# Moving an output layer's first sums and an x^T load to earlier places in a fused attention and squared-ReLU kernel

## The chip, the cores and the metric

The kernel runs on one core of a Trainium2 chip. The core has five engines with a queue each: TensorE (PE, matrix products), VectorE (DVE), ScalarE (ACT), GpSimd (POOL) and SyncE (SP, which here issues nearly all DMAs). Each engine takes its instructions strictly in the order in which the program gives them, and waits on semaphores for the others. The metric is device time in microseconds (us); lower is better.

## The reference

Two blocks one after the other, all in float32:

```python
scores = q @ k.T / 8                      # 8 x 8 heads, 576 positions, head size 64
scores = where(scores >= max(scores) - tau, scores, -1e9)
attn   = exp(scores - max) / (sum + 1e-9)
x      = (attn @ v), heads side by side   # 4608 x 512
h      = maximum(x @ w_in, 0)             # w_in 512 x 2048
out    = (h * h) @ w_out                  # w_out 2048 x 512, out 4608 x 512
```

## The kernel before

**Attention.** 32 pairs of heads, each cut into five blocks of queries, give 160 *slots*. `slot(n)` is a pipeline written out by hand: it mixes stages of several neighbouring blocks (scores of block n + 3, softmax of n + 1 and n + 2, transposes of n - 1, products with the values of n - 2). The result of a block is copied from PSUM by ACT (L418, L421) into one of three buffers `xr` and stored as x^T to DRAM by SP (queued in `later`, issued by `ask()`, L547). Between the slots of attention lie side jobs: from slot 0 the output weights are fetched and converted, from slot 35 POOL makes sums of them (`sums`, L130), which SP stores in groups of seven tiles (`keep`, also L547); from slot `IN_FIRST` = 76 the input weights follow (fetch at L181, conversion at L201 to L239). At slot 76 SP is also asked for x^T of the first token step, `load_x(0)` (L641, four DMAs of 256 KB), and from slot 78 on POOL makes one sum of it in every third slot (`prepare_x`, L130). That x^T lies in a region of its own.

**Both layers of the feed-forward part** use a Winograd form of Strassen's scheme two levels deep: 7 outer times 7 inner products for each step of 512 tokens (9 steps), 49 *products* of four matmuls. The price are sums and differences of blocks, before the products (of the operands) and after them (of the results). The outer loop runs over `OUTER` = (1, 2, 6, 7, 4, 5, 3); I call the place in that loop *index* 0 to 6. Within an index, `inner` makes seven products (1, 6, 7, 5, 2, 4, 3) into four PSUM banks out of a ring of six, with a *tick* after each (0 to 6):

```python
        product(X, 1, False); copy(p1, X);          tick(0)
        product(Y, 6, False); u2 = Y + p1;          tick(1)
        product(Z, 7, False); u3 = Z + u2;          tick(2)
        product(W, 5, False); final((1,1), W, u3);  tick(3)
        product(X, 2, True);  final((0,0), X, None); tick(4)
        product(Z, 4, True);  final((1,0), Z, u2);  tick(5)
        product(W, 3, True);  final((0,1), W, u2);  tick(6)
```

(shortened). The last three products add into banks that `p1`, `u3` and the first `final` must have read before.

*Hidden layer* (`hidden_layer`, products at L708): DVE makes the sums that read PSUM (L133); POOL makes a second addition for most results (L133, one for each of three results in an index, two in index 5). A finished block goes to ACT four ticks later: ReLU (L687), square (L688), and SP stores it to DRAM as `g` (L689).

*Output layer* (`output_layer`, products at L843): its operands are `g` blocks, loaded back by `load_g` (L786). Sums of them come in two kinds. `outer_sums(n, o, ks)` give the blocks (o, k) for outer products o = 5, 6, 3, 7; each is made by `sum_v`: ACT copies one operand to a PSUM bank `c` (L654), and DVE adds or subtracts (L133, L130). `inner_sums(n, m)` give (m, 5), (m, 6), (m, 3) on POOL and (m, 7) by `sum_v`. I write (5,7) for the outer sum with o = 5 and k = 7.

**The last step of the hidden layer** (n = 8) has no next x^T to prepare. It is used for step 0 of the output layer: `load_g(0, ...)` asks for the 16 blocks of m = 7, 4, 1, 2 at its start; a table `work` gives sums by index, and `spread(work, at)` spreads the list of an index over its seven ticks; in the same ticks `reload` (L940) brings the output weights back into the tiles of the input weights. In the output layer, `work_of(i)` gives the sums to be made during index i. The first copy of that layer, `p1` of index 0 (L622), goes into a buffer that was a hidden-layer `U2` block until POOL's last addition has read it.

Of the kernel before, what the change touches and what calls it, by code (L numbers as in the profile page):

```python
# [48 lines left out]
def kernel(  # L49
# [218 lines left out]
    def load(i):  # L268
        b, hp = pairs[i]
        h = 2 * hp  # L270
        qn = sb.tile([P, FULL, P], FP32, tag="qn", name="qn")
        kn = sb.tile([P, FULL, P], FP32, tag="kn", name="kn")

        rn = sb.tile([P, P], FP32, tag="rn", name="rn")

        for src, dst, order, rows in ((q, qn, "(t p) d -> p t d", 0), (k, kn, "(p t) d -> p t d", REST)):

            queue = nc.scalar if i == 0 and src is k else nc.sync
            for j in range(2):
                queue.dma_start(out=dst[:, :, ds(j * D, D)], in_=src[b, h + j, 0:MAIN, :].rearrange(order, p=P))  # L280
            queue.dma_start(
                out=rn[ds(rows, REST), :].rearrange("p (j d) -> p j d", j=2),
                in_=src[b, h : h + 2, MAIN:S, :].rearrange("j p d -> p j d"),
            )
        loaded[i] = (qn, kn, rn)
# [164 lines left out]
    def turn_part(n, part):  # L450

        if n < 0:
            return
        if n not in rows_of:
            transposes(n)
        rows_of[n][part]()
# [22 lines left out]
    def give_x(n, xr):  # L479
        i, t = slots[n]  # L480
        b, hp = pairs[i]
        later.append((xT[b][ts(hp, P), ds(t * P, BLK[t])], xr[:, 0, 0 : BLK[t]]))
# [51 lines left out]
    IN_FIRST = OUT_SUMS + 41  # L534
# [240 lines left out]
    def operand(n, m, k):  # L775
        at = PLACE[(28 * n + 4 * KINDS.index(m) + K_ORDER.index(k)) % 36]
        operands[n, m, k] = arena[:, ds(at, BANK)].rearrange("p (k t) -> p k t", k=4)
        return operands[n, m, k]

    def load_g(n, kinds):  # L780

        for m, k in kinds:
            row, col = next((a, b) for a in range(2) for b in range(2) if AT_A[a][b] == m)
            a, b = next((a, b) for a in range(2) for b in range(2) if AT_A[a][b] == k)
            j = 4 * (2 * col + b) + 2 * row + a
            nc.sync.dma_start(out=operand(n, m, k), in_=gT[n][j][:, :].rearrange("p (k t) -> p k t", k=4))  # L786
# [9 lines left out]
    def outer_g(n, o, k):  # L796
        op, x, y = SUM_OF[o]
        x, y = operands[n, x, k], operands[n, y, k]
        sum_g(nc.vector, op, operands[n, o, k] if o == 7 else operand(n, o, k), x, y)

    def inner_g(n, m, o):
        op, x, y = SUM_OF[o]
        x, y = operands[n, m, x], operands[n, m, y]
        if o != 7:
            operands[n, m, o] = fin.tile([P, 4, NQ], FP32, tag="gi")
        sum_g(nc.vector if o == 7 else nc.gpsimd, op, operands[n, m, o], x, y)

    def inner_sums(n, m):
        return [lambda o=o: inner_g(n, m, o) for o in (5, 6, 3, 7)]

    def outer_sums(n, o, ks=K_ORDER):
        return [lambda k=k: outer_g(n, o, k) for k in ks]
# [72 lines left out]
    with tc.manual_schedule():  # L885
        with ExitStack() as stack:
            sc_pool = stack.enter_context(tc.tile_pool(name="sc", bufs=2, space=PSUM))
            b_pool = stack.enter_context(tc.tile_pool(name="b", bufs=2, space=PSUM))

            def bank(shape, name):  # L890
                return b_pool.tile(shape, FP32, tag="b", name=name)

            def keep_busy(times):

                pt = bank([P, P], "idle")
                for _ in range(times):
                    nc.tensor.transpose(pt[:, :], ident[:, :], ident[:, :])

            load(0)
            load_v(0)  # L900
            keep_busy(10)
            for _ in turn(0):
                pass
            turn_last(0, bank([P, P], "pqkr")[:, :])()
            load_v(1)
            for n in range(-3, len(slots)):
                slot(n)
                if -3 < n < 0:
                    keep_busy(12)
                if n == IN_FIRST:  # L910
                    load_x(0)
                    xsums = prepare_x(0, lambda op, out, x, y: op(nc.gpsimd, out, x, y))
                if n > IN_FIRST + 1 and n % 3 == 0:
                    next(xsums, None)
            n = len(slots)

            def drain():

                while pending:
                    pt, m, of = pending.popleft()  # L920
                    xr = sb.tile([P, 2, P], FP32, tag="xr", bufs=3)
                    nc.scalar.copy(xr[:, 0, 0:m], pt[:, 0, 0:m])
                    give_x(of, xr)

            drain()
            values_and_load(n - 2)
            for part in "RWw":
                turn_part(n - 1, part)
            values_and_load(n - 1)
            drain()  # L930
            for _ in range(60):
                sums_step()
            ask()
        banks = ctx.enter_context(tc.tile_pool(name="banks", bufs=1, space=PSUM))

        def reload(at):

            m, k = OUTER[at // 7], INNER[at % 7]
            t = weight_tile(W_OUT, m, k)
            nc.sync.dma_start(out=t[:, :], in_=w_dram[m, k][:, :])  # L940

        for n in range(NSTEP):
            last = n == NSTEP - 1
            if not last:
                load_x(n + 1)
                xsums = prepare_x(n + 1, sum_v)
            else:
                load_g(0, [(m, k) for m in (7, 4, 1, 2) for k in K_ORDER])
                work = {
                    3: [*outer_sums(0, 5, (7,)), *outer_sums(0, 6, (7,))],  # L950
                    4: [*outer_sums(0, 3, (7,)), *outer_sums(0, 7, (7,))],
                    5: inner_sums(0, 1),
                    6: outer_sums(0, 5, (1, 2)) + outer_sums(0, 7, (1,)),
                }

            def also(m, at):
                i = OUTER.index(m)
                if not last:
                    if 2 <= i <= 5 and at < 6:
                        next(xsums)  # L960
                    return
                spread(work.get(i, []), at)
                if 7 * i + at > 9:
                    reload(7 * i + at - 10)

            hidden_layer(n, also)
            if not last:
                next(xsums, None)
        for n in range(NSTEP):
            more = n + 1 < NSTEP  # L970

            def work_of(i):

                work = [] if i == 6 else inner_sums(n, OUTER[i + 1])
                if (n, i) == (0, 0):
                    work += outer_sums(0, 6, (1, 2)) + outer_sums(0, 5, (4,)) + outer_sums(0, 6, (4,))
                if (n, i) == (0, 1):
                    work += outer_sums(0, 7, (2, 4)) + outer_sums(0, 3, (1, 2, 4))
                if more and i == 4:
                    work += outer_sums(n + 1, 5)  # L980
                if more and i == 5:
                    work += outer_sums(n + 1, 6) + outer_sums(n + 1, 7, (7, 1))
                if more and i == 6:
                    work += outer_sums(n + 1, 3) + outer_sums(n + 1, 7, (2, 4)) + inner_sums(n + 1, 1)
                return work

            def also(m, at):
                i = OUTER.index(m)
                if n == 0 and 7 * i + at < 10:
                    reload(39 + 7 * i + at)  # L990
                if more and (i, at) == (2 if n == 0 else 0, 0):
                    load_g(n + 1, [(m_, k) for m_ in KINDS[0:2] for k in K_ORDER])
                if at == 0:
                    work[0] = work_of(i)
                spread(work[0], at)
                if at > 4:
                    squares_due(0)
                if at == 2:
                    ask()
                if at == 6:  # L1000
                    if more and i == (2 if n == 0 else 0):
                        load_g(n + 1, [(7, k) for k in K_ORDER])
                    if more and i == (2 if n == 0 else 1):
                        load_g(n + 1, [(4, k) for k in K_ORDER])

            work = [None]
            output_layer(n, also)
        ask()
# [36 lines left out]
```

## Time and profile before

| | |
|---|---|
| median of 7 runs | 1465.62 us (1465.27 to 1467.18) |
| profiled execution | 1465.27 us, of it span 1463.5 us |
| PE busy | 1435.8 us, 98% of the span |
| POOL, DVE, ACT busy | 1053.2, 1007.1, 889.8 us |
| DMA | 176.90 MB, mean 121 GB/s |
| attention | 0 to 662.9 us |
| hidden layer | 662.9 to 1061.1 us, nine steps of 44 us |
| output layer | 1061.1 to 1460 us, nine steps of 44 us |

A busy time is the time in which the engine had an instruction under way. The stages follow one another on PE, and each has another set of helpers, so a wait has to be read in its own stage. "A <- B" in the profile means that A was released by B. In the tables of groups and waits, a line such as L133 is a helper's line (`plus`; `minus` is L130), so the tile names tell the uses apart: `ph` is a hidden-layer product, `po` one of the output layer, `arena` the big SBUF region, `c` the bank of `sum_v`.

### The profile page before, as it was taken

How to read it: one execution, taken by the hardware profiler on the slowest of the kernel's cores; microseconds unless marked ns; L12 is line 12 of the kernel's file. 1: busy time of each engine (PE TensorE's matmuls, PEld its weight loads, DVE VectorE, ACT ScalarE, POOL GpSimd, SP SyncE). 2: the span in 40 equal slices, each digit the busy share in tenths (PEclk: the TensorE clock that was granted, in tenths of full speed). 3: DMA queues.
4: the chain of work that ended last, by engine and by line, in shares of the span. 5: the costliest groups of instructions: out<-in, count | busy, mean ns of one | idle time of the engine just before them, and what ended most of it. 6: DMA issues, size and time to landing. Idle time of an engine off the chain costs nothing. (4 is left out here: it accounts for less than half of the span.)

```text
span 1463.5 us, 35324 instructions
## 1 busy us (share of the span) xinstructions
PE 1435.8 (98%) x12914; PEld 1216.1 (83%) x12914; DVE 1007.1 (69%) x2152; ACT 889.8 (61%) x1792; POOL 1053.2 (72%) x1318
## 2 busy tenths in 40 slices
PE   8999999999999999999999999999999999999998
PEld 5666666666666666669999999999999999999998
DVE  4888766777887667666777877777765666545663
ACT  5888777777887777774766665766553333322330
POOL 3777788878888888773556655566677777777775
PEclk9999999999999999999999999999999999999999
DMA  4343223566442222202433233433984432244411
GB/s 126 106 128 112 62 65 114 163 231 205 123 122 75 54 55 65 64 26 63 144 127 128 93 112 120 145 123 127 386 294 145 144 130 78 88 140 144 145 30 30
DMA packets 212957, 176.90 MB, mean 121 GB/s; under 512 B 99888, under 2 KB 161328, under 8 KB 212784
## 3 DMA queue, kind: packets, MB, share of 16 engines
q1 hardware_dynamic: 210896, 174.09, 37.6%
q8 instruction: 102, 1.67, 0.5%
q10 hardware_dynamic: 1888, 0.56, 0.2%
q14 instruction: 71, 0.58, 0.1%
HBM read 105.12 MB, written 69.47 MB: 119 GB/s over the span
## 5 line engine op out<-in xcount | busy, mean ns | idle before, releaser
L133 POOL TENSOR_TENSOR arena<-arena 128x512 f32<-128x512 f32 (+1 forms) x314 | 376.9, 1223 | 252.4 <-DVE arena L133 208.4
L708 PE MATMUL ph<-arena,w 128*128 128x128 f32 x3528 | 396.6, 275 | 2.1 <-DVE arena L133 1.1
L843 PE MATMUL po<-w,arena 128*128 128x128 f32 x3528 | 396.3, 275 | 2.1 <-ACT arena L622 1.8
L708 PEld LDWEIGHTS ph<-arena,w 128*128 128x128 f32 x3528 | 394.7, 192 | 4.0 <-DVE arena L133 3.5
L843 PEld LDWEIGHTS po<-w,arena 128*128 128x128 f32 x3528 | 394.7, 192 | 3.6 <-ACT arena L622 2.0
L133 DVE TENSOR_TENSOR arena<-ph,arena 128x512 f32<-128x512 f32 x378 | 255.7, 688 | 94.0 <-PE ph L708 53.4
L366 DVE TENSOR_REDUCE arena<-sc 128x1 f32<-128x576 f32 x288 | 217.5, 755 | 127.5 <-PE sc L355 127.3
L383 DVE SCALAR_TENSOR_TENSOR arena<-sc,arena 128x576 f32<-128x576 f32 x288 | 224.6, 814 | 7.2 <-ACT arena L378 7.0
L398 POOL TENSOR_SCALAR arena<-arena 128x576 f32<-128x576 f32 (+1 forms) x320 | 223.5, 708 | 7.4 <-DVE arena L389 2.6
L133 DVE TENSOR_TENSOR arena<-po,arena 128x128 f32<-128x128 f32 x378 | 108.2, 290 | 169.7 <-PE po L843 166.5
L654 ACT COPY c<-arena 128x512 f32<-128x512 f32 (+1 forms) x303 | 172.7, 579 | 61.5 <-DVE arena L130 56.4
L378 ACT ACTIVATE arena<-sc,arena 128x576 f32<-128x576 f32 x288 | 200.7, 747 | 10.6 <-DVE arena L366 6.4
L439 PEld LDWEIGHTS pwT<-ident,arena 128*128 128x128 f32 x1152 | 128.5, 141 | 77.0 <-issue 29.9
L355 PE MATMUL sc<-arena 64*128 64x512 f32 (+2 forms) x768 | 184.5, 571 | 1.1 <-DVE arena L383 0.7
L130 POOL TENSOR_TENSOR arena<-arena 128x512 f32<-128x512 f32 (+1 forms) x138 | 175.0, 1268 | 11.8 <-DMA arena<-xT 2.1
L439 PE MATMUL pwT<-ident,arena 128*128 128x128 f32 x1152 | 181.0, 280 | 1.2 <-ACT arena L311 0.7
L130 DVE TENSOR_TENSOR arena<-arena,c 128x512 f32<-128x512 f32 (+1 forms) x267 | 174.8, 663 | 6.9 <-ACT c L654 6.3
L441 ACT COPY arena<-pwT 128x512 f32<-128x512 f32 x256 | 151.4, 592 | 41.8 <-PE pwT L439 31.6
L469 PE MATMUL pvR<-arena 128*64 128x128 f32 (+1 forms) x2560 | 163.3, 268 | 5.1 <-ACT arena L441 0.7
L469 PEld LDWEIGHTS pvR<-arena 128*64 128x64 f32 x2560 | 127.8, 136 | 34.9 <-issue 20.6
L687 ACT ACTIVATE arena<-arena 128x512 f32<-128x512 f32 x144 | 89.9, 624 | 77.6 <-POOL arena L133 77.6
L622 ACT COPY arena<-po 128x128 f32<-128x128 f32 x63 | 16.7, 265 | 180.1 <-PE po L843 178.1
(56 smaller groups left out, 1157.0 us busy)
## 6 DMA issues: line engine op xcount, KB each, us to landing
g<-arena SPq DMA_DIRECT2D x144, 256.0 KB, 2.0
arena<-g SPq DMA_DIRECT2D x144, 256.0 KB, 4.3
w<-w SPq DMA_DIRECT2D x98, 256.0 KB, 4.8
out_dram<-arena SPq DMA_DIRECT2D x70, 128.0 KB, 2.3
arena<-in_q_dram SPq DMA_DIRECT2D x64, 128.0 KB, 2.6
arena<-in_v_dram SPq DMA_DIRECT2D x32, 256.0 KB, 2.8
arena<-in_moe_w_out_dram SPq DMA_DIRECT2D x16, 512.0 KB, 4.1
xT<-arena SPq DMA_DIRECT2D x128, 64.0 KB, 1.5
```

The lines of the kernel that those rows point to most:

```text
L130: e.tensor_tensor(out=out, in0=x, in1=y, op=ALU.subtract)
L133: e.tensor_tensor(out=out, in0=x, in1=y, op=ALU.add)
L355: nc.tensor.matmul(to, qT[rows, ds(t * P, m)], kT[rows, ds(k0, n)], start=True, stop=True)
L366: nc.vector.tensor_reduce(out=nmx[:, j : j + 1], in_=sc[:, ds(at[j], S)], axis=AXIS.X, op=ALU.max, negate=True)
L378: nc.scalar.activation(out=w[:, ts(j, S)], in_=sc[:, ds(at[j], S)], func=AF.Exp, bias=nmx[:, j : j + 1], scale=1.0)
L383: nc.vector.scalar_tensor_tensor(out=w[:, ts(j, S)], in0=sc[:, ds(at[j], S)], scalar=thr[:, j : j + 1], in1=w[:, ts(j, S)], op0=ALU.is_ge, ...
L398: nc.gpsimd.tensor_scalar(out=out, in0=w, scalar1=r, scalar2=1.0, op0=ALU.mult, op1=ALU.mult)
L439: nc.tensor.transpose(pt[:, c, :], w[:, ds(j * (S + REST) + c * P, P)], ident[:, :])
L469: nc.tensor.matmul(pv[rows, :], va[:, j, c, :], wT[:, j, c, 0:n], start=(c == 0), stop=False, skip_group_check=True)
L654: nc.scalar.copy(c, y)
L708: nc.tensor.matmul(to[:, j, :], W_IN[m, k][:, ts(j, P)], of[k][:, m - 1, :], start=(not more and j == 0), stop=True, skip_group_check=True,)
L843: nc.tensor.matmul(to, g[:, j, :], w[:, j, :], start=(not more and j == 0), stop=(j == 3), skip_group_check=True)
```

## The change

It has two parts. The load of the first step's x^T is asked for after slot 64 instead of after slot 76; the sums of it stay in their slots. And in the last hidden step the sums for output step 0 are placed anew: the four outer sums with k = 7 go from indices 3 and 4 to 2 and 3; the inner sums of m = 1 go from index 5 to 4; index 5 has none; in index 6, (5,1) and (5,2) stay at ticks 2 and 4, the entries `rest` being empty; (7,1) leaves index 6 for index 1 of the output layer, ahead of (7,2) and (7,4).

```diff
-                if n == IN_FIRST:
+                if n == IN_FIRST - 12:
                     load_x(0)
                     xsums = prepare_x(0, lambda op, out, x, y: op(nc.gpsimd, out, x, y))
...
                 load_g(0, [(m, k) for m in (7, 4, 1, 2) for k in K_ORDER])
+                rest = lambda: None
+                first, second_one = outer_sums(0, 5, (1, 2))
                 work = {
-                    3: [*outer_sums(0, 5, (7,)), *outer_sums(0, 6, (7,))],
-                    4: [*outer_sums(0, 3, (7,)), *outer_sums(0, 7, (7,))],
-                    5: inner_sums(0, 1),
-                    6: outer_sums(0, 5, (1, 2)) + outer_sums(0, 7, (1,)),
+                    2: outer_sums(0, 5, (7,)) + outer_sums(0, 6, (7,)),
+                    3: outer_sums(0, 3, (7,)) + outer_sums(0, 7, (7,)),
+                    4: inner_sums(0, 1),
+                    6: [rest, rest, first, rest, second_one, rest, rest],
                 }
...
                 if (n, i) == (0, 1):
-                    work += outer_sums(0, 7, (2, 4)) + outer_sums(0, 3, (1, 2, 4))
+                    work += outer_sums(0, 7, (1, 2, 4)) + outer_sums(0, 3, (1, 2, 4))
```

## The prediction

> **What bounds the kernel now.** I read the page first. TensorE (PE) is busy 1435.8 of 1463.5 us, at a granted clock of 0.9 or more in every slice, so no other engine's busy time buys anything; what can be won is PE's idle time, 27.7 us in all, and only where the changed lines cause it. Second, the waits of PE, whose columns are the total in us, the number of waits and the longest. I keep those that fall next to the edits.
>
> ```profile
> PE po L843 <- ACT arena L622: 1.8, 1, 1.8
> PE ph L708 <- DVE arena L133: 1.1, 1, 1.1
> PE pqk L306 <- ACT arena L418: 1.1, 1, 1.1
> PE pwT L439 <- ACT arena L311: 0.7, 1, 0.7
> PE pvR L469 <- ACT arena L309: 0.3, 1, 0.3
> ```
>
> Each occurs once. The first two lie at the seam of hidden and output layer (1059 to 1067 us), where the sums are moved; the other three follow each other within 7 us of attention (339 to 346 us), just after the load that is moved. Third, the timeline of both places (start, duration; in brackets the idle time before and its releaser). Around the load:
>
> ```profile
> 331.95 2.13 SPq L641 DMA_DIRECT2D arena<-xT  x4
> 334.49 0.33 SPq L547 DMA_DIRECT2D xT<-arena  x1
> 339.31 0.37 ACT L418 COPY arena<-pvR 128x256 f32<-128x256 f32 x1 [2.73 <-DMA xT<-arena]
> 339.74 0.66 PE L306 MATMUL pqk<-ident,arena 128*128 128x128 f32 x4 [1.09 <-ACT arena L418]
> 342.64 0.66 PE L439 MATMUL pwT<-ident,arena 128*128 128x128 f32 x4 [0.74 <-ACT arena L311]
> 346.06 0.69 PE L469 MATMUL pvR<-arena 128*64 128x64 f32 x16 [0.32 <-ACT arena L309]
> ```
>
> SP issues in order. The four loads of x^T (1 MB) stand ahead of an x^T store whose data ScalarE (ACT) had ready at 325.3. The store goes out at 334.49 and lands 4.7 us later, at 339.2; the `xr` ring has three buffers, so the copy that reuses that buffer (due at 339.31 - 2.73 = 336.58) stands still for 2.73 us, and PE loses 1.09 + 0.74 + 0.32 = 2.15 us while ACT catches up. Around the seam:
>
> ```profile
> 1056.92 0.63 ACT L687 ACTIVATE arena<-arena 128x512 f32<-128x512 f32 x1 [0.56 <-POOL arena L133]
> 1058.12 0.58 ACT L654 COPY c<-arena 128x512 f32<-128x512 f32 x1
> 1058.81 0.69 DVE L133 TENSOR_TENSOR arena<-arena,c 128x512 f32<-128x512 f32 x1 [1.74 <-ACT c L654]
> 1060.15 1.16 PE L708 MATMUL ph<-arena,w 128*128 128x128 f32 x8 [1.13 <-DVE arena L133]
> 1060.60 0.63 ACT L687 ACTIVATE arena<-arena 128x512 f32<-128x512 f32 x1 [1.90 <-POOL arena L133]
> 1066.37 0.27 ACT L622 COPY arena<-po 128x128 f32<-128x128 f32 x1 [2.00 <-POOL arena L133]
> 1066.68 3.50 PE L843 MATMUL po<-w,arena 128*128 128x128 f32 x29 [1.80 <-ACT arena L622]
> ```
>
> This is one chain, read from the top: a late GpSimd (POOL) add holds a ReLU on ACT; the copy to `c` for an output-layer sum queues behind it; VectorE (DVE) waits for `c` with the hidden layer's own sum behind it; PE waits 1.13. The same again, then POOL's last add frees the buffer of the first `p1` copy of the output layer, and PE waits 1.80. POOL is late because in index 5 (m=5) it has six adds of its own and three inner sums: 9 x 1.25 = 11.2 us in an index of seven products of 44.01 / 49 = 0.898, 6.3 us.
>
> **The change part by part.** No instruction is added or taken away; the eleven sums of the work table keep their operations, nine of them move. Each DVE sum is an ACT copy (0.55 to 0.59) and a DVE operation (0.62 to 0.69), each POOL sum 1.25.
>
> *The load.* Four DMAs leave SP at slot 76 and enter at slot 64, with a slot of 4.0 us. On the changed SP queue they stand behind a group of seven weight stores (273.81 to 277.67) and before two x^T stores. Removed at 332: the store goes out at 331.95 instead of 334.49, with 1 MB less in front of it. This case's ordinary x^T stores land in 1.5 to 2.7 us, so at 333.5 to 334.7, and even the 4.1 us of a crowded store gives 336.1, before 336.58. The stall goes: -2.15. POOL's first x^T sum, which waited 2.1 us for this load, no longer waits; PE did not wait for that. Added at 277.8: SP is blocked for 2.1 to 2.5 us; the store now issued at 277.77 goes out at about 280.2, behind the rest of the weight stores (the DMA engines are busy until 279.5) and 1 MB more at some 380 GB/s, 2.8 us, so it lands near 282.3 + 2 = 284.3. Its buffer is wanted three copies later, at 288.81: 4.5 us to spare. The next store (issued about 281) needs to land by 293.0. SP then waited until 284.58 for the v load, 3.2 us after it was through, so the q, k and v loads are not moved. Cost 0.
>
> Here two rules speak, one against the edit. The Trainium skill, "DMA: Bandwidth & Descriptors", section "Anatomy of one DMA — SWDGE (gpsimd) path", gives a DMA about 2.0 us of constant fixed cost plus its bytes over 436 GB/s. The page fits it for GpSimd's path, but taken as the law for a 32 KB store, it would land at 334.49 + 2.1 = 336.6, ACT would not have waited, and moving the load would be worth 0. The row says 4.7 us, because the store's data wait behind the loads; the row decides, and the sum has 2.15. In the same page, section "Queues, rings and completion order", descriptors are consumed in ring order: that is the reason why the stores behind the load at slot 64 must pay too, 2.8 us each as used above. By that rule the stall could simply move; by the rows of that place it has 4.5 us of room.
>
> *The sums.* In index 2 now come (5,7) and (6,7), in index 3 (3,7) and (7,7), in index 4 the inner sums, in index 5 none, in index 6 as before (5,1), (5,2) at ticks 2 and 4, while (7,1) goes to index 1 of the output layer.
> - Index 5: POOL has 6 x 1.25 = 7.5 us instead of 11.2. Index 4 takes 6 x 1.25 = 7.5 as well, on a POOL that idled 2.00 us there. It starts index 5 on time (1052) and has the (1,0) output ready at about 1055.9 instead of 1056.9, the (0,1) output at 1058.4 instead of 1060.58.
> - First wait: ACT has the ReLU at 1056.36, the moment it is free, instead of 1056.92. Copy, sum and PE follow 0.56 sooner: 1.13 becomes 0.57. It does not go, since (5,1) and (5,2) stay where they are.
> - Second wait: ReLU and square of (0,1) run from 1058.7 to 1059.9; `c` for (5,2) is there at 1060.4 (before: 1062.4), the DVE sum at 1061.0, the product sums at 1061.7 and 1062.3, POOL's two adds until about 1064.4, the `p1` copy until 1064.7. PE, started 0.56 sooner, ends its four products at 1064.3 and goes on at about 1064.6 instead of 1066.68. So the second wait becomes 0.3, and PE is 2.1 us earlier in all.
> - Cover of the sums moved up: at tick 3 of index 2 ACT is still in squares until 1033.72, so `c` is ready at 1034.2 and the sum at 1034.9; five DVE operations behind it run until 1038.6, and PE's product that needs the last of them starts at 1039.3. 0.7 us remain; if that cover is gone, PE pays the excess. The operands are there: the 16 g loads go out from 1018.7 to 1028.1 and land in 2.9 to 6.0 us; the latest one needed in index 2 is the ninth.
> - Index 1 of the output layer gets a seventh copy and sum, 0.55 on ACT and 0.62 on DVE. In the trace of before the next `p1` copy ends at 1078.15 and is needed at 1079.25; DVE is level again at 1079.8, and PE needs it at 1081.0. Both hold 0.6 more. Cost 0, up to 0.5 if I misread an order.
> - SP's queue keeps its order in the last step; the reload of weights (DMA busy share 1.05 until 1073) runs some 30 us ahead of its use.
>
> Bounds, per edit: the load between +1 (a new stall of half the size) and -3.0 (the three waits and a wait of 0.91 at 356.5 on DVE, which I count as staying: there POOL has an x^T sum, a conversion and two small copies in a row). The sums between +0.5 and -2.93 (both waits gone). Sum taken: -2.15 - 2.1 = -4.25. Profiled execution: 1465.27 (span 1463.5 and 1.8 around it), so 1461.0; the median of the runs is 0.35 above the profiled one, so 1461.4.
>
> **The rivals.**
> 1. Only one edit pays. Either the store stall comes from the crowd of weight stores and q, k, v loads on SP and not from x^T (for: those alone held SP from 321.45 to 331.9; against: 331.95 plus 4.1 is in time), or the seam's waits only change their releaser. Then 1463.2 to 1463.5.
> 2. Both pay fully, the 0.91 with them, and the first seam wait vanishes: -2.15 - 0.9 - 2.9 gives 1459.7.
> 3. Slower: the new place of the load makes a store stall of its own. Place: the ACT copy at 288.8. Price: PE paid 2.15 for an ACT wait of 2.73, so 0.8 per us. It decides once the store lands after 288.8, and outweighs the gains (4.25 / 0.8 = 5.3 us) only if it lands after 294.1, nearly 14 us after its issue, or if the old stall stays too (2.1 / 0.8 = 2.6 us, landing after 291.4). The longest landing seen near is 5.6 us. Then about 1466.
> 4. The edit does nothing in effect, because PE gives the time back at the next tight place: no later PE wait in the output layer is listed, so PE has nothing to give it back to.
>
> **How the numbers follow.** A difference under 0.2% (2.9 us) is about what a measurement of this kernel can't tell from no change. Forecast (gain 3 to 5.2): 0.62. Rival 2: 0.10. Rival 1: 0.18, within 0.2%. Rival 3: 0.06; rival 4: 0.04. Faster by over 0.2%: 0.62 + 0.10 = 0.72; the same: 0.18 + 0.04 = 0.22; slower: 0.06. The range from 1459.8 to 1463.6 takes in the forecast, most of rival 2 and rival 1.
>
> **What would show it.** Right: no ACT wait on an x^T store near 336, four L641 issues near 278, hidden layer beginning 2.1 us sooner (662.9 to 660.8); in the seam, index 5 on POOL without a subtraction, PE's wait on L708 at 0.6 and on L843 at 0.3. Wrong: an ACT wait on xT near 289, a PE wait on L708 in indices 2 to 4, a PE wait on L843 in index 2 of the output layer, or the 339 us waits still there.

## The result, and the profile after

The changed kernel takes 1461.58 us (median of 15 runs, 1461.13 to 1462.13) against 1465.59 us of the kernel before, measured with it (35 runs). The ratio is 0.9972, 95% interval 0.9965 to 0.9978: 4 us less. The profiled execution has a span of 1460.0 us, 3.5 less than before: the hidden layer begins 1.35 sooner (at 661.55 instead of 662.90), and from there to the end it takes 798.46 us instead of 800.58, 2.12 less. That execution was late from its first slots on: just ahead of the old stall the same product starts at 329.91 in it and at 329.37 before. The stretch from there to the hidden layer is 1.9 shorter.

First the waits of PE in the changed kernel, those next to the edits (total in us, number, longest; the view lists waits of 0.15 us and more):

```profile
PE ph L708 <- DVE arena L133: 0.5, 1, 0.5
PE pvR L469 <- ACT arena L309: 0.3, 1, 0.3
```

Of five waits two are left. The waits of 1.8 on `po`, of 1.1 on `pqk` and of 0.7 on `pwT` are no longer in the list, and 1.1 on `ph` has become 0.5.

The timeline around both places of the load, of the changed kernel:

```profile
274.35 3.87 SPq L547 DMA_DIRECT2D w<-w  x7
278.26 2.49 SPq L641 DMA_DIRECT2D arena<-xT  x4
280.85 1.11 SPq L547 DMA_DIRECT2D xT<-arena  x2
285.13 0.38 SPq L292 DMA_DIRECT2D arena<-in_v_dram  x1
289.35 0.37 ACT L418 COPY arena<-pvR 128x256 f32<-128x256 f32 x1 [0.77 <-PE pvR L414]
...
333.48 0.34 SPq L547 DMA_DIRECT2D xT<-arena  x1
337.39 0.37 ACT L418 COPY arena<-pvR 128x256 f32<-128x256 f32 x1 [0.27 <-PE pvR L414]
344.69 0.69 PE L469 MATMUL pvR<-arena 128*64 128x64 f32 x16 [0.32 <-ACT arena L309]
```

At the new place the load stands behind the seven weight stores and ahead of two x^T stores, and SP is through before the next v load is due. The ACT copy at 289.35, which reuses the buffer of the first delayed store, waits for PE and not for a DMA. At the old place the store that was late is followed by no stall: the copy at 337.39 waits for PE. Its landing, from the DMA view of 331.9 to 334.8 us of the changed kernel (size, us from issue to landing):

```profile
xT<-arena SPq DMA_DIRECT2D x1, 32.0 KB, 2.3
```

So it landed at 335.8; before it was 4.7 us, and 339.2.

The seam of the changed kernel:

```profile
1054.93 0.61 ACT L687 ACTIVATE arena<-arena 128x512 f32<-128x512 f32 x1
1056.11 0.58 ACT L654 COPY c<-arena 128x512 f32<-128x512 f32 x1
1056.79 0.69 DVE L133 TENSOR_TENSOR arena<-arena,c 128x512 f32<-128x512 f32 x1 [1.07 <-POOL arena L133]
1058.14 1.16 PE L708 MATMUL ph<-arena,w 128*128 128x128 f32 x8 [0.47 <-DVE arena L133]
1059.13 396.94 PE L843 MATMUL po<-w,arena 128*128 128x128 f32 x3528
1062.58 0.27 ACT L622 COPY arena<-po 128x128 f32<-128x128 f32 x1 [1.75 <-POOL arena L133]
```

The ReLU ahead of the first `c` copy no longer waits for POOL (it had 0.56 before); that copy, the sum and PE follow, and PE's wait shrinks from 1.13 to 0.47. The `p1` copy still waits for POOL's last addition, but it ends at 1062.85, when PE is just finishing the four products it needs no `p1` for (at 1062.87). The output layer then runs without a listed wait: 396.94 us for all its products, against 398.40 before. That is 1.46 less, although a wait of 1.80 went; where the other 0.3 went is seen below, with (7,1) alone.

### The profile page after: what moved, and what is told of

Same layout as the page of the kernel before. It is cut to its first block, busy times and chain, and to the rows that moved or that the text cites. A ratio compares the mean times of both kernels' runs of the same rounds, so it can differ in the third digit from the quotient of the medians.

```text
span 1460.0 us, 35321 instructions
## 1 busy us (share of the span) xinstructions
PE 1435.2 (98%) x12914; PEld 1215.4 (83%) x12914; DVE 1007.0 (69%) x2152; ACT 890.1 (61%) x1792; POOL 1053.5 (72%) x1318
## 5 line engine op out<-in xcount | busy, mean ns | idle before, releaser
L469 PE MATMUL pvR<-arena 128*64 128x128 f32 (+1 forms) x2560 | 163.3, 268 | 5.1 <-ACT arena L441 0.7
L469 PEld LDWEIGHTS pvR<-arena 128*64 128x64 f32 x2560 | 127.8, 136 | 34.9 <-issue 20.8
```

The source lines that it names most:

```text
L469: nc.tensor.matmul(pv[rows, :], va[:, j, c, :], wT[:, j, c, 0:n], start=(c == 0), stop=False, skip_group_check=True)
```

## The experiments

All were measured with rounds of the kernel before on the same chip; "ratio" is to that kernel. Medians of different groups are compared with care, since the kernel before itself had medians of 1465.29, 1466.8 and 1465.53 in them.

**The load alone** (kernel before, `if n == IN_FIRST - 12: load_x(0)`).

> The kernel before with only the load moved to slot 64. Theory (the store stall is the load's doing, and the two edits add up): the waits of 1.09 and 0.74 on PE near 340 go, the one of 0.32 stays, as in the changed kernel, so 1465.6 - 1.9 = 1463.7 us; the seam keeps its waits of 1.1 and 1.8. Rival (the stall comes from the crowd of weight stores and q, k, v loads alone, and went by another cause): 1465.6 and an ACT wait on an x^T store near 337.

1463.51 us, ratio 0.9989 (0.998 to 0.9998). No stall near 337, the wait of 0.32 kept, the seam unchanged:

```profile
1058.02 1.16 PE L708 MATMUL ph<-arena,w 128*128 128x128 f32 x8 [1.13 <-DVE arena L133]
1064.56 15.68 PE L843 MATMUL po<-w,arena 128*128 128x128 f32 x138 [1.81 <-ACT arena L622]
```

The load is worth 1.6 to 1.8 us, by ratio and by medians (the interval of the ratio is 0.3 to 2.9).

**The sums alone** (changed kernel with `if n == IN_FIRST: load_x(0)`).

> The changed kernel with the load back at slot 76. Theory (edits independent): PE waits 0.5 on L708 at the seam and nothing on L843, but keeps 1.09, 0.74 and 0.32 near 340: 1465.6 - 2.1 = 1463.5 us. Rival (the gain at the seam comes from a shift that the load brings to the DMA queue): 1465 or more.

1462.76 us, ratio 0.9982 (0.9973 to 0.999), 2.5 us less than before by the medians, with an interval of 1.5 to 4.0. In its trace the time from the start of the hidden layer to the end is 798.41 us against 800.58, so 2.2 less. The seam is as in the changed kernel (0.46, then nothing); near 340 PE waits 0.50, 0.73 and 0.32. The two edits lie in stages that don't touch, and 1.8 + 2.5 = 4.3 is the 4.0 of both within the intervals.

**The inner sums alone, late in index 4.**

```diff
-                    4: [*outer_sums(0, 3, (7,)), *outer_sums(0, 7, (7,))],
-                    5: inner_sums(0, 1),
+                    4: [*outer_sums(0, 3, (7,)), *outer_sums(0, 7, (7,)), *inner_sums(0, 1)],
```

> The kernel before with only the inner sums of m=1 moved from index 5 to index 4, behind the two outer sums of that index. Theory (POOL's three sums in index 5 are the whole cause): the seam's waits become 0.5 and 0 as with all sums moved, 1463.5 us. Rival (the ACT copies and DVE sums had to be moved up too, or (7,1) away from tick 6): one of the two waits stays at over 1 us, 1464.3 us or more, or a new PE wait on L708 appears in index 4, where ACT and DVE get three sums.

1464.52 us, ratio 0.9992 (0.9983 to 1.0001). The simple theory fell. Index 5 is rid of the three sums, and yet PE waits longer at the first place than before:

```profile
1058.56 1.16 PE L708 MATMUL ph<-arena,w 128*128 128x128 f32 x8 [0.30 <-DVE arena L133]
1061.29 1.16 PE L708 MATMUL ph<-arena,w 128*128 128x128 f32 x8 [1.57 <-DVE arena L133]
1066.24 14.00 PE L843 MATMUL po<-w,arena 128*128 128x128 f32 x123 [0.22 <-ACT arena L622]
```

POOL's own rows say why:

```profile
1041.27 2.50 POOL L133 TENSOR_TENSOR arena<-arena 128x512 f32<-128x512 f32 x2 [0.53 <-DVE arena L133]
1046.38 2.51 POOL L133 TENSOR_TENSOR arena<-arena 128x512 f32<-128x512 f32 x2 [2.61 <-DMA w<-w]
```

The list puts the inner sums at ticks 3, 4 and 5. POOL, in order, sits idle for 2.61 us in index 4 (from 1043.8 to 1046.4, before the first result of that index is due; the releaser named there can't be it: what follows is an addition of results), and then has six additions to do with too little time. It carries the delay into index 5.

**The same three sums at ticks 1, 3 and 5**, with (3,7) and (7,7) between them, (5,7), (6,7) and (7,1) left where they were. ("e1's sibling" in the expectation is the kernel just shown.)

```diff
+                    4: [j for p in zip(inner_sums(0, 1), outer_sums(0, 3, (7,)) + outer_sums(0, 7, (7,))) for j in p]
+                    + inner_sums(0, 1)[2:],
```

> The kernel before with only the inner sums of m=1 moved to index 4, now with POOL's three at ticks 1, 3 and 5 and the outer sums (3,7), (7,7) between them at ticks 2 and 4; (5,7) and (6,7) stay in index 3, (7,1) in index 6. Theory (what counts is that POOL has work in its idle stretch at the start of index 4; e1's sibling with the inner sums at ticks 3 to 5 left that stretch empty): waits of 0.5 and 0 at the seam, 2.1 to 2.5 us below the kernel before, ratio 0.9983. Rival (ACT and DVE have to be relieved in index 4 as well): one wait over 1 us stays, ratio 0.999 or more.

1463.03 us, ratio 0.9978 (0.9969 to 0.9987). POOL and PE of this kernel:

```profile
1041.03 3.73 POOL L133 TENSOR_TENSOR arena<-arena 128x512 f32<-128x512 f32 x3 [0.53 <-DVE arena L133]
1045.78 1.27 POOL L133 TENSOR_TENSOR arena<-arena 128x512 f32<-128x512 f32 x1 [1.02 <-ACT c L654]
1059.38 1.16 PE L708 MATMUL ph<-arena,w 128*128 128x128 f32 x8 [0.46 <-DVE arena L133]
1064.28 15.90 PE L843 MATMUL po<-w,arena 128*128 128x128 f32 x140 [0.17 <-ACT arena L622]
```

One more addition now fills POOL's idle stretch (three in a row from 1041.03 instead of two). That alone gives all of the first wait's gain and all but 0.17 of the second. From the start of the hidden layer to the end this kernel takes 798.20 us, the kernel just shown 799.99 and the changed kernel 798.46. The outer sums with k = 7 did not have to move to other indices for it, and (7,1) did not have to leave index 6. (Within index 4 the two outer sums stand one and two ticks later here than in the kernel just shown; that this did not matter is read from POOL's rows, not tried alone.)

**(7,1) alone** to index 1 of the output layer (kernel before, index 6 with `[rest, rest, first, rest, second_one, rest, rest]`).

> The kernel before with only (7,1) moved from tick 6 of index 6 to index 1 of the output layer. Theory: (7,1) stands behind the last hidden-layer sum on DVE and ahead of the p1 copy on ACT, but that copy waits for POOL, so nothing is gained: 1465.6 us within 0.3, waits of 1.1 and 1.8 as before. Rival (the copy for (7,1) ahead of p1 is what makes PE wait 1.8): the second wait shrinks by 0.6 or more, 1465.0 us or less.

1465.3 us, ratio 0.9998 (0.9989 to 1.0007): the waits are 1.12 and 1.81, nothing is gained. The trace shows a small loss, which the times can't resolve: the products of the output layer take 398.72 us, against 398.40 before. PEld, the weight loads of PE, show where, in index 2 (kernel before, this kernel, changed kernel):

```profile
1075.83 10.35 PEld L843 LDWEIGHTS po<-w,arena 128*128 128x128 f32 x92
1079.77 4.32 PEld L843 LDWEIGHTS po<-w,arena 128*128 128x128 f32 x38 [0.18 <-DVE arena L133]
1076.62 3.54 PEld L843 LDWEIGHTS po<-w,arena 128*128 128x128 f32 x31 [0.19 <-DVE arena L133]
```

With a seventh sum in index 1, DVE comes later to its additions of index 2, and PE waits for one of them. By the starts of the matmuls around it PE loses 0.3 us in all, in steps that are too small for the list of PE's waits. The kernels that leave (7,1) in index 6 have no such step.

**The load one slot later**, after slot 77, behind the store that was late; POOL's sums of it begin at slot 81.

> The kernel before with the load asked for one slot later (after slot 77), so that it stands behind the one x^T store that was late, in the same crowd of weight stores and q, k, v loads; POOL's sums begin one turn later (slot 81). Theory (the load delays that store, by SP's order and by its bytes ahead of it): the store goes out near 332 and lands in under 3 us, no ACT wait on it near 337; the next two stores now stand behind the load and may wait a little near 341; 1463.5 to 1464.5 us. Rival (the crowd as such makes stores slow, wherever the load stands): the ACT wait near 337 stays at 1.5 or more, 1465 us or more.

1463.34 us, ratio 0.9987 (0.9979 to 0.9996): as good as at slot 64. The store now lands 2.1 us after its issue. SP and ACT of this kernel:

```profile
333.09 0.52 SPq L547 DMA_DIRECT2D xT<-arena  x1
334.13 2.17 SPq L641 DMA_DIRECT2D arena<-xT  x4
337.44 0.37 ACT L418 COPY arena<-pvR 128x256 f32<-128x256 f32 x1 [0.27 <-PE pvR L414]
341.47 0.27 ACT L421 COPY arena<-pvR 128x128 f32<-128x128 f32 x1 [0.53 <-DMA xT<-arena]
```

The same megabyte in the same crowd costs PE no wait here, once the store goes out ahead of the load. The next store waits in its place, but for 0.53 on ACT, which PE does not feel. The 0.32 on L469 is gone as well; POOL makes no sum in slot 78 here, which may be the reason, but was not tried alone.

**The load spread** over slots 73 to 76, one DMA each.

> The kernel before with the same four DMAs of the load asked for one by one, after slots 73, 74, 75 and 76. Theory (it is the 1 MB in one piece ahead of the store that costs): only 256 KB and 0.6 us of SP stand ahead of the late store, so most of the stall goes, PE keeps under 0.5 of the 1.8 near 340: 1463.7 to 1464.3 us. Rival (it is the sum of bytes in the busy stretch from 316 to 345): stall as before, 1465 us or more.

1464.43 us, ratio 0.9992 (0.9983 to 1.0001), runs from 1463.1 to 1466.2: the time does not decide it. The trace does for the stall. ACT at 336.96 waits 0.28 for PE and for no DMA, PE has only the 0.32 left, and the hidden layer begins at 661.03 (660.81 with the load at slot 64). The profiled execution lost its gain elsewhere: its window table has a granted clock below 1 in the output layer, and a finer one shows that the loss lies in one place, just behind the seam. The third row is the same place in the kernel before. (Each row: us, then busy time and count of PE, PEld, DVE, ACT, POOL, then the clock, DMA share and GB/s.)

```profile
1060.00:1200.00 140.00, 138.11 (x1216) 137.44 (x1215) 84.18 (x211) 55.79 (x115) 106.91 (x90) 0.99 0.50 167
1066.00:1070.00 4.00, 4.00 (x24) 4.00 (x23) 2.67 (x6) 3.95 (x8) 2.24 (x2) 0.59 1.05 391
1068.00:1072.00 4.00, 4.00 (x38) 4.00 (x37) 3.03 (x7) 3.94 (x9) 2.20 (x2) 1.00 1.05 394
```

**What is still there: (5,1) and (5,2) out of index 6** (changed kernel).

```diff
-                    6: [rest, rest, first, rest, second_one, rest, rest],
+                    5: [rest, rest, rest, rest, rest, first, second_one],
```

> The changed kernel with (5,1) and (5,2) moved from ticks 2 and 4 of index 6 to ticks 5 and 6 of index 5, so that index 6 has no sums. Theory (the last seam wait of 0.5 comes from (5,1) standing ahead of a hidden-layer sum on DVE): no PE wait at the seam, 0.5 us below the changed kernel, ratio to the kernel before 0.9969. Rival (index 5 has no room on ACT, which has the squares of index 4 there): the squares and the p1 copy of index 6 come 1.1 us later, a PE wait on L708 of 0.3 or more at the start of index 6, ratio 0.9972 or above.

1460.96 us, ratio 0.9962 (0.995 to 0.9975). The seam has no wait; one row holds all hidden-layer products:

```profile
661.33 396.94 PE L708 MATMUL ph<-arena,w 128*128 128x128 f32 x3528 [0.30 <-ACT arena L922]
```

**The second x^T sum in slot 82 instead of 81** (changed kernel, `n % 3 == 0 and n != 81 or n == 82`). In the changed kernel POOL has in a row:

```profile
349.55 1.26 POOL L130 TENSOR_TENSOR arena<-arena 128x512 f32<-128x512 f32 x1
350.89 0.66 POOL L215 TENSOR_SCALAR arena<-arena 128x512 f32<-128x512 f32 x1
355.14 0.49 PE L340 MATMUL sc<-arena 128*128 128x128 f32 x2 [0.91 <-DVE arena L383]
```

> The changed kernel with the second x^T sum on POOL in slot 82 instead of slot 81. Theory (the wait of 0.91 near 355, the same before and after, is POOL's pile in slots 81 and 82: x^T sum, conversion, two small copies in a row): that wait goes, 0.9 us below the changed kernel, ratio 0.9966. Rival (it is a leftover of the fetches and has nothing to do with that sum, or moves to slot 83): ratio 0.9972, a wait of about 0.9 at 355 or 359.

1460.92 us, ratio 0.9961 (0.9948 to 0.9975). The sum now comes later, and PE's wait is gone:

```profile
349.52 0.65 POOL L215 TENSOR_SCALAR arena<-arena 128x512 f32<-128x512 f32 x1
353.61 1.27 POOL L130 TENSOR_TENSOR arena<-arena 128x512 f32<-128x512 f32 x1
353.90 0.39 PE L340 MATMUL sc<-arena 128*128 128x128 f32 x2
```

**Both.**

> The changed kernel with both further edits, (5,1) and (5,2) in index 5 and the x^T sum in slot 82. Theory (they are in different stages, so they add up): 1.4 us below the changed kernel, ratio 0.9963, both waits gone. Rival (one of them moves its wait): 0.9966 to 0.9972.

1459.77 us, ratio 0.9955 (0.9942 to 0.9967), with neither wait: the fastest version measured here. In that group the kernel before ran at 1466.8, so the ratios of these three, and of the kernel with the sums at ticks 1, 3 and 5, flatter them by almost 0.001; the medians stand 0.6, 0.7 and 1.8 below the changed kernel's 1461.58.

## Why the prediction was right, point by point

- *The sum.* Forecast 1461.4, measured 1461.58. The main reasons are the stated ones, each shown by doing one part alone: load 1.6 to 1.8 (forecast 2.15), sums 2.1 to 2.2 by the traces and 2.5 by the medians (forecast 2.1). That the sums come so close to 2.1 is luck in part: the second seam wait went further down than foreseen, by about 0.3, and a cost of 0.3 that was put at 0 took it back.
- *The load, removed at 332.* Shown: with the load elsewhere (slot 64, slot 77, or in pieces) the ACT wait on the store is gone. The hidden layer was to begin at 660.8; it does with the load alone (660.81), and at 661.55 in the changed kernel, whose profiled execution was 0.54 late before that place. The term was mis-sized in two ways. The wait of 0.32 was counted as part of the stall, but stays in the changed kernel, with no stall in front of it. And the stall was taken from one execution: in the profiles with the load at slot 76 the first PE wait was 1.09, 0.50, 1.52, 0.26 and 0.92, the second 0.73 or 0.74 each time. Their mean, 0.86 + 0.73 = 1.6, is what the load alone gave by its ratio.
- *The load, added at 278.* SP was blocked 2.49 (2.1 to 2.5 foreseen), the two stores behind it took 4.1 us to land where they had taken 2.0, so the first did at 284.9 (284.3), with 4.4 us to spare (4.5). No cost, as said; rival 3 did not occur.
- *The two rules against the row.* A fixed 2 us, the first of the two rules that the prediction weighs, would have made the load's move worth nothing. The store took 4.7 us behind the load and 2.3 without it, and the load alone is 1.6 to 1.8 us faster: the row was right. The order on SP's queue decides: with the store ahead of the load the wait was gone. It acts twice, by a later issue (334.49 instead of 331.95) and by a longer landing. By an estimate from these rows neither alone would have cost more than about 0.2, since 334.49 + 2.3 and 331.95 + 4.7 are 336.8 and 336.65, and the copy was due at 336.58.
- *The first seam wait.* 0.57 forecast, 0.47 measured. That (5,1) ahead of the hidden-layer sum keeps it alive is shown by the kernel that moves it.
- *The second seam wait.* 0.3 forecast, none listed: the `p1` copy ends at 1062.85 and PE's four products at 1062.87. The forecast had that copy end at 1064.7, which is 1063.35 once the 1.35 us are taken off by which the layers begin sooner: 0.5 too late. The two seam waits together gave 0.66 + 1.80 = 2.46, not 2.1.
- *Why POOL is late.* The prediction counted nine additions against six in index 5. That is only half of it: six in index 4 are harmless if one of them falls in POOL's 2 us of idle time there, and harmful if not (1.8 us between the two kernels that differ in this). The text named that idle time and used it without calling it decisive.
- *The cover of the sums moved up.* No PE wait in indices 2 to 4, cost 0 as said.
- *The seventh sum in index 1 of the output layer.* Cost 0 forecast, 0.3 measured, inside the "up to 0.5" that the prediction allowed. It read one product too far: the first one that needs DVE's additions starts at 1080.19 in the trace of before, not at 1081.0. So 2.46 of waits became 2.12 us. With only the inner sums moved, at ticks 1, 3 and 5 of index 4, the gain in the layers was 2.4 (798.20 against 800.58).
- *The wait of 0.91* was counted as staying, and stayed; its cause was named rightly, as the sum in slot 82 shows.

## What to carry to other kernels

On an engine that works in order, ask for a side job just before a stretch in which the engine would wait; removing work from the full stage is not enough. Here the same three additions in the same index cost 1.8 us more when they came after that stretch. A store that guards a small ring of buffers should not stand behind a large load on the same queue: try their order before looking for bandwidth. When the bound engine is 98% busy, go through its few single waits in order of time and ask for each what stands ahead of the releaser.

## What the runs showed that I had not expected

The landing time of one 32 KB store went from 4.7 to 2.3 us with the load out of its way, and the stall that it caused varied by more than 1 us between executions of the same code (first PE wait 0.26 to 1.52).

A wait of PE may cost more than its length. In the profile of the spread load the granted clock drops about 1.1 us after PE comes back from its wait of 1.81 at the seam, and stays down for some 3.4 us: the matmuls start 0.213 us apart instead of 0.111. From that wait on, the output layer takes 394.43 us instead of 392.85, 1.6 us longer, as much as the edit that it was to measure. In the lists of runs, 49 of the 112 runs of kernels that keep the wait of 1.8 have a mean granted clock below 1.000, and 3 of the 63 of kernels without it; on one and the same chip it was 9 of 14 against 0 of 25. With the load alone, runs at 0.998 took 1464.58 us in the median and runs at 1.000 1463.45. So the sums may save a little beyond the waits that a single profile shows. That the wait brings the drop about is not shown: only one trace has caught it, and no experiment was made for it.
